# Four transformer layers on one core: the stores of the residual stream and of the output are begun from SyncE's queue instead of ScalarE's

## The chip, the cores and the metric

The kernel runs on one core of a Trainium2 chip. A core has five engines that work side by side: PE (TensorE, matrix products), DVE (VectorE), ACT (ScalarE), POOL (GpSimd) and SP (SyncE, which computes nothing and only begins transfers). A transfer between the chip's memory and a core's on-chip memory is begun by an instruction on the queue of SP, ACT or POOL, and is carried out by 16 DMA engines that all queues share. Each engine's queue runs in order: an instruction that waits holds up everything queued behind it on that engine.

The metric is the time of one execution in microseconds (us).

## The reference

Input `x` has 2048 rows (tokens) of 640 numbers, 32 heads of 20 numbers each. Two kinds of layer alternate, A B A B, and each adds its result to the residual stream `x`:

```python
x = A_x
x = x + _A_ref(_layernorm(x), A_wqkv, A_wo)          # linear attention
x = x + _B_ref(_layernorm(x), B_wq, ..., B_beta)     # segments with a memory
x = x + _A_ref(_layernorm(x), A_wqkv, A_wo)
x = x + _B_ref(_layernorm(x), B_wq, ..., B_beta)
# A: pq, pk = phi(q), phi(k); kv = pk^T v;  o = (pq kv) / (pq . sum(pk)), then @ wo
# B: per segment of 512 tokens and head
logits = qs @ ks^T * scale + mask;  a_dot = softmax(logits) @ vs
o = g * (pq @ M) / (pq . z) + (1 - g) * a_dot        # M, z: memory of earlier segments
M = M + pk^T vs;  z = z + sum(pk)                    # then o @ wo
```

## The kernel before, in words

The 2048 tokens are worked on in four segments of 512, and a segment in four tiles of 128 rows. The residual stream lives in the chip's memory: each layer loads a tile of it (`x` or `xo`), adds the layer's result into a new tile `xn`, and stores `xn`. A store is 128 x 640 numbers of 4 bytes, 320 KB, and there are 16 of them in each of the four layers, 64 in all. The last layer's 16 go to the output `out_x`, the other 48 to buffers that the next layer reads.

The stores stand in two places. In `a_second` (line 828, layers A, 32 stores) VectorE makes `xn` from the product in PSUM and the old `x` (line 479). In `b_out` (line 976, layers B, 32 stores) ScalarE copies the product (line 476) and GpSimd adds the old `x` (line 477); only for the last segment of the last layer does VectorE do both at once. Both stores use the queue `q_x`:

```python
self.o_half(oT[i], wo, "B", x, xn, n, later=not st.get("ends"))
...
self.q_x.dma_start(dst[r:r + P], xn)
```

Two streams of work are woven together. `dense` makes the projections, the residual additions and the memory; `attention` goes through the heads of layer B in groups of four, eight groups to a segment, 32 to a layer, 64 in the kernel. A group's work is spread over three slots: `row_max` (scores, then row maxima on VectorE, line 1013); `split_max` and `max_rows`, which turn the maxima into rows (transposed on PE in line 1031, copied by ScalarE into `mt` in line 1033) and send them by two small transfers into the query stack `qs` (line 1036, a pair of 4 KB transfers on SyncE's queue); then `scores` (PE in line 1048, exponential on ScalarE in line 1052, causal mask on GpSimd in line 1059) and `weigh` (PE, line 1075). The scores of a group cannot begin before its row pair has landed. The stacks `qs` and `ks` of the next group are loaded a group ahead (`stacks`, line 993), also on SyncE's queue.

PE's order of work is written out by hand: `run` steps the two streams by a planned cost, and `MANUAL = ("PE",)` keeps PE's instructions as they were written. The order on the other engines and queues is laid out when the program is built, by estimated times and dependencies.

Which queue begins which transfer is set by one tuple. Its six entries are, in order: the stored queries of layer A (`q_pq`), the stores of the residual stream and of the output (`q_x`), the queries and keys of layer B (`q_nat`), the row pair (`q_row`), the weights (`q_w`), and the reload of layer A's queries (`q_pqi`). Loads of the residual stream (line 330) and of the stacks (line 993) are on SyncE's queue in any case.

```python
self.q_pq, self.q_x, self.q_nat, self.q_row, self.q_w, self.q_pqi = [getattr(self.nc, e) for e in QUEUES]
```

Of the kernel before, what the change touches and what calls it, by code (L numbers as in the profile page):

```python
# [142 lines left out]
class Kernel:  # L143
    def __init__(self, ctx, tc, A, const, out):
# [7 lines left out]
        self.rate = 1.0  # L152
        self.q_pq, self.q_x, self.q_nat, self.q_row, self.q_w, self.q_pqi = [getattr(self.nc, e) for e in QUEUES]

# [1170 lines left out]

ROWS = 11
PQ = 5
QUEUES = ('gpsimd', 'scalar', 'sync', 'sync', 'gpsimd', 'sync')
PE_BUFS = 10
MANUAL = ("PE",)  # L1330
_INS = ["A_x", "A_wqkv", "A_wo", "B_wq", "B_wk", "B_wv", "B_wo", "B_beta"]
# [31 lines left out]
```

## Time and profile before

| what | value |
|---|---|
| median of three runs | 1738.13 us (1735.6 to 1741.74) |
| the profiled execution's own time | 1736.07 us |
| its span, first to last instruction | 1734.4 us |
| granted TensorE clock | 0.998 |
| PE busy | 1666.1 us, 96% |
| ACT busy | 969.7 us, 56% |
| transfers | 187.58 MB, 108 GB/s over the span |

The profile comes from one execution. "Busy" is the time in which an engine worked; the sequencer's own instructions (starting transfers, waiting on semaphores) are not counted in it and are shown with a q behind the engine's name: SPq, ACTq. L976 is line 976 of the kernel. In a row of the timeline stand the start, the duration, the engine, the line, the operation, what is written and read, how many instructions were merged, and in brackets the idle time before it with what ended it. In a row of windows stand the window, its length, PE's busy time in it, the granted clock, the DMA engines' busy share and GB/s. In a row of one source line stand the engine, the operation, the count, the shortest, median and longest duration in ns, and the first and last start in us. In a row of waits stand the total, the number of times and the longest.

### The profile page before, as it was taken

What the parts mean: (1) busy time and instruction counts of PE and PEld (TensorE: products, weight loads), DVE (VectorE), ACT (ScalarE), POOL (GpSimd) and SP (SyncE); (2) the same over time, 40 slices, a digit from 0 to 9 for tenths busy, and PEclk for the clock granted to TensorE, in tenths of its full rate; (3) what the DMA queues carried; (4) which work ended last, traced back from release to release, by engine and by line L of the source; (5) the groups of instructions that cost most, each with busy time, mean ns of one, the idle gap of its engine ahead of it and who ended that gap; (6) DMA issues with size and microseconds to landing.
All of it is one profiled execution on the core that took longest, in us unless ns stands there. A gap on an engine that the chain in (4) does not pass through costs nothing.

```text
span 1734.4 us, 36014 instructions
## 1 busy us (share of the span) xinstructions
PE 1666.1 (96%) x13032; PEld 1047.5 (60%) x13032; DVE 1180.9 (68%) x3849; ACT 969.7 (56%) x1818; POOL 517.7 (30%) x982
## 2 busy tenths in 40 slices
PE   6999999999999999999999999999999999999998
PEld 4676667664565576556556777666546545645555
DVE  8645534577787677759864456746777877878773
ACT  5545433357557645667675544333665576666673
POOL 1543350012123312334351301221422432233452
PEclk9999999999999999999999999999999999999999
DMA  7522452422322322352211303423232323223432
GB/s 262 184 109 95 150 195 97 139 76 82 113 71 73 113 96 68 120 179 95 78 48 51 103 32 122 175 98 116 75 102 85 112 81 108 93 82 111 131 115 92
DMA packets 118330, 187.58 MB, mean 108 GB/s; under 512 B 13949, under 2 KB 79613, under 8 KB 115849
## 3 DMA queue, kind: packets, MB, share of 16 engines
q1 hardware_dynamic: 105896, 142.68, 25.5%
q0 software_dynamic: 3040, 21.63, 3.4%
q10 hardware_dynamic: 9216, 20.98, 3.1%
q8 instruction: 103, 1.69, 0.4%
q14 instruction: 75, 0.61, 0.1%
HBM read 106.05 MB, written 78.64 MB: 106 GB/s over the span
## 4 chain that ended last, share of the span: by engine, by line
PE 78%; DVE 10%; ACT 6%; issue 2%; POOL 2%; DMA 1%; SPq 1%; ACTq 0%; POOLq 0%; DVEq 0%
PE ps L395 32%; PE ps L381 17%; PE ps L1075 7%; PE ps L1048 4%; ACT pe L1052 3%; PE ps L1007 3%; PE ps L319 3%; PE ps L564 3%; PE ps L450 3%; DVE ps L1013 2%; PE ps L1088 1%; PE ps L891 1%; PE ps L730 1%; DVE st L338 1%; DVE xn L479 1%
## 5 line engine op out<-in xcount | busy, mean ns | idle before, releaser
L1013 DVE CUSTOM_DVE_ANT_0 ps<-ps,maskw 128x512 f32<-128x512 f32 (+3 forms) x1024 | 472.5, 519 | 38.0 <-PE ps L1007 35.7
L1052 ACT ACTIVATE pe<-ps,lsc 128x512 f32<-128x512 f32 x640 | 394.8, 696 | 87.6 <-PE ps L1048 84.9
L1059 POOL TENSOR_SCALAR_AFFINE_SELECT pe<-pe 128x256 f32<-128x256 f32 (+1 forms) x640 | 229.7, 365 | 449.2 <-ACT pe L1052 444.0
L395 PEld LDWEIGHTS <-xT 128*128 128x128 f16 x2880 | 280.3, 98 | 114.6 <-issue 9.3
L395 PEld LDWEIGHTS <-oT 128*128 128x128 f16 x1920 | 185.7, 98 | 80.5 <-issue 7.0
L1075 PE MATMUL ps<-pe,v 128*32 128x512 f32 (+3 forms) x2048 | 162.2, 436 | 11.5 <-POOL pe L1059 5.1
L395 PE MATMUL ps<-w_Bo,oT 128*128 128x320 f16 x960 | 142.3, 302 | 2.8 <-ACT pe L1052 1.1
L1013 DVE DVE_READ_ACCUMULATOR2_ANT mg<- 128x1 f32 x1024 | 143.9, 141 | 0.0
L381 PE MATMUL ps<-xT,w_Bq 128*128 128x512 f16 x600 | 140.2, 380 | 1.9 <-ACT pe L1052 0.8
L395 PE MATMUL ps<-w_Bv,xT 128*128 128x320 f16 x960 | 139.7, 300 | 0.8 <-DVE otok L1095 0.6
L381 PE MATMUL ps<-xT,w_Bk 128*128 128x512 f16 x600 | 138.8, 380 | 1.2 <-ACT pe L1052 1.2
L395 PE MATMUL ps<-w_Ak,xT 128*128 128x320 f16 x960 | 136.1, 300 | 0.0
L1007 PE MATMUL ps<-ks,qs 60*128 60x512 f16 (+3 forms) x1024 | 123.1, 298 | 6.7 <-ACT pe L1052 2.9
L856 DVE SCALAR_TENSOR_TENSOR nat<-ps,nat 128x512 f16<-128x512 f32 x80 | 55.2, 690 | 89.2 <-ACT nat L855 89.1
L1048 PE MATMUL ps<-qs,ks 62*128 62x512 f16 (+3 forms) x1024 | 105.9, 301 | 3.0 <-DMA qs<-mt 1.5
L1075 PEld LDWEIGHTS ps<-pe,v 128*32 128x32 f32 x2048 | 65.3, 109 | 71.9 <-issue 45.8
L421 POOL TENSOR_SCALAR e<-e 128x320 f32<-128x320 f32 (+1 forms) x52 | 82.9, 1594 | 82.4 <-ACT e L417 78.2
L855 ACT ACTIVATE nat<-ps 128x512 f16<-128x512 f32 x80 | 48.2, 603 | 91.8 <-PE ps L381 69.2
L381 PEld LDWEIGHTS <-w_Bk 128*128 128x128 f16 x600 | 57.3, 98 | 65.5 <-issue 5.6
L381 PEld LDWEIGHTS <-w_Bq 128*128 128x128 f16 x600 | 56.7, 98 | 65.9 <-issue 7.8
L1007 PEld LDWEIGHTS <-qs 60*128 60x128 f16 x1024 | 50.0, 94 | 70.9 <-issue 44.7
L343 POOL TENSOR_TENSOR rs<-rs,mhalf 128x1 f32<-128x1 f32 x48 | 27.0, 563 | 218.8 <-DVE rs L342 218.7
(217 smaller groups left out, 2630.7 us busy)
## 6 DMA issues: line engine op xcount, KB each, us to landing
x<-xn ACTq DMA_DIRECT2D x48, 320.0 KB
qs<-qd SPq DMA_DIRECT2D x128, 120.0 KB
ks<-kd SPq DMA_DIRECT2D x128, 120.0 KB
xo<-x SPq DMA_DIRECT2D x48, 320.0 KB
pqi<-pqd SPq DMA_DIRECT2D x32, 320.0 KB
qd<-nat SPq DMA_DIRECT2D x40, 256.0 KB
kd<-nat SPq DMA_DIRECT2D x40, 256.0 KB
x<-in_A_x SPq DMA_DIRECT2D x16, 320.0 KB
```

The source lines that it names most:

```text
L319: nc.tensor.transpose(pt[:, (c - c0) * P:(c - c0 + 1) * P], src[:, c * P:(c + 1) * P], self.ident)
L381: nc.tensor.matmul(p, w[:, c, a, t * P:(t + 1) * P], xT[:, c, b, :], start=k == 0, stop=k == 3 * C - 1)
L395: nc.tensor.matmul(p, xT[:, c, a, i * P:(i + 1) * P], w[:, c, b, n * HN:(n + 1) * HN], start=k == 0, stop=k == 3 * C - 1)
L421: nc.gpsimd.tensor_scalar(e, e, 1.0, eps, op0=OP.min, op1=OP.add)
L450: nc.tensor.matmul(nd[:, lo - k * cut:hi - k * cut], pq[t], mem[:, OFF[t] + lo - a:OFF[t] + hi - a], start=first, stop=True, skip_group_ch ...
L856: nc.vector.scalar_tensor_tensor(nat[:, 1], p, QK_SHIFT, nat[:, 0], op0=OP.mult, op1=OP.subtract)
L1007: nc.tensor.matmul(bs[par][:, a:a + n], qs[r, p, i * P:(i + 1) * P], ks[r, p, :n], start=True, stop=True)
L1013: nc.vector.tensor_tensor_reduce(bs[par][:, a:a + n], bs[par][:, a:a + n], self.maskw[:, SEG - n:], 1.0, NEG, OP.add, OP.max, G["mg"][:, p ...
L1048: nc.tensor.matmul(b[:, a:a + n], ks[r, p, j * P:(j + 1) * P], qs[r, p, j * P:], start=True, stop=True)
L1052: nc.scalar.activation(e, b, AF.Exp, scale=self.lsc)
L1059: nc.gpsimd.affine_select(d, d, pattern=pat, compare_op=OP.is_ge, fill=0.0, base=0, channel_multiplier=-1)
L1075: nc.tensor.matmul(G["pv"][32 * h4:32 * h4 + 32, j * P:], v[j][:, h * E1:h * E1 + 32], G.pop((p, par, j)), start=j == 0, stop=j == 2, skip ...
```

## The change

One entry of the tuple goes from `'scalar'` to `'sync'`. The 64 stores are begun by SyncE, from the queue that also carries the loads, the queries and keys of layer B and the row pairs.

```diff
 ROWS = 11
 PQ = 5
-QUEUES = ('gpsimd', 'scalar', 'sync', 'sync', 'gpsimd', 'sync')
+QUEUES = ('gpsimd', 'sync', 'sync', 'sync', 'gpsimd', 'sync')
 PE_BUFS = 10
 MANUAL = ("PE",)
```

## The prediction

> **What bounds the kernel now.** I read the head of the profile page first: busy times, DMA queues, the chain of work that ended last, and the issues of the tensors whose store is moved.
>
> ```profile
> span 1734.4 us, 36014 instructions
> PE 1666.1 (96%) x13032; PEld 1047.5 (60%) x13032; DVE 1180.9 (68%) x3849; ACT 969.7 (56%) x1818; POOL 517.7 (30%) x982
> ...
> q1 hardware_dynamic: 105896, 142.68, 25.5%
> ...
> q10 hardware_dynamic: 9216, 20.98, 3.1%
> ...
> PE 78%; DVE 10%; ACT 6%; issue 2%; POOL 2%; DMA 1%; SPq 1%; ACTq 0%; POOLq 0%; DVEq 0%
> ...
> x<-xn ACTq DMA_DIRECT2D x48, 320.0 KB
> out_x<-xn ACTq DMA_DIRECT2D x16, 320.0 KB
> ```
>
> PE is busy 96% of the span; 1734.4 - 1666.1 = 68.3 us is all that it does not work. The change touches no matmul, so 68.3 us is the whole room for a gain. ScalarE's queue (ACTq) has 0% of the chain that ended last, SyncE's queue (SPq) 1%. The 64 stores are the only 20.98 MB on q10: 64 x 320 KB agrees, so q10 is ScalarE's row of DMA work and q1 is SyncE's, which already carries 142.68 MB.
>
> The profiled execution took 1736.07 us, its span 1734.4; the median of the runs is 1738.13, 2.06 above it, and the three runs lie 6 us apart. About 0.3%, 5.2 us, is what a measurement of this kernel can tell from no change, and "the same" means that below.
>
> **What a store costs on ScalarE.** Next come the stores by source line, and the timeline of one of them on four engines.
>
> ```profile
> L828 ACTq DMA_DIRECT2D x<-xn x32: 325/326/369, 261.8 to 1496.6; - x32
> L976 ACTq DMA_DIRECT2D x<-xn x16: 326/326/359, 556.7 to 978.2; - x16
> L976 ACTq DMA_DIRECT2D out_x<-xn x16: 338/338/374, 1608.6 to 1731.2; - x16
> ```
>
> ```profile
> 717.60 1.27 ACT L1052 ACTIVATE pe<-ps,lsc 128x512 f32<-128x512 f32 x2
> 718.79 0.33 ACTq L976 DMA_DIRECT2D x<-xn  x1
> 719.22 0.27 ACT L1033 ACTIVATE mt<-pm 32x128 f16<-32x128 f16 x1 [0.35 <-POOL pe L1059]
> 719.51 1.28 SPq L1036 DMA_DIRECT2D qs<-mt  x2
> 717.80 0.96 POOL L477 TENSOR_TENSOR xn<-xn,xo 128x320 f32<-128x320 f32 x1 [2.95 <-ACT xn L476]
> 722.90 0.61 PE L1048 MATMUL ps<-qs,ks 62*128 62x512 f16 x4
> ```
>
> The store begins at 718.79, right after GpSimd's add ended (717.80 + 0.96 = 718.76). It takes 0.33 us of ScalarE's sequencer, not of its datapath. The activation behind it starts at 719.22 although the one before had ended at 717.60 + 1.27 = 718.87: 0.35 us of ScalarE are lost, and the row pair on SyncE's queue (the row maxima that the scores need) begins 0.35 us later than it could. PE reads those rows at 722.90 and shows no wait there.
>
> **Part one, what leaves ScalarE.** 64 stores at 326 to 338 ns (their medians) are 32 x 0.326 + 16 x 0.326 + 16 x 0.338 = 21.1 us of issuing. What counts is only what PE later waits for. So I asked for PE's busy time in the 3 us behind each store that has 3 us behind it (63 windows; two of them and the sum are shown).
>
> ```profile
> 1636.21:1639.21 3.00, 1.18 (x9) 0.96 0.85 302
> 1674.44:1677.44 3.00, 1.92 (x16) 1.00 0.77 286
> sum 189.00, PE 182.67; mean PE 2.90
> ```
>
> In all 63 windows PE is idle 189.00 - 182.67 = 6.33 us. That is the upper bound of a direct gain. Two windows hold 1.82 + 1.08 = 2.90 us of it. There I looked at ScalarE and PE:
>
> ```profile
> 1635.50 0.69 ACT L1052 ACTIVATE pe<-ps,lsc 128x512 f32<-128x512 f32 x1
> 1636.21 0.34 ACTq L976 DMA_DIRECT2D out_x<-xn  x1
> 1636.65 1.84 ACT L1052 ACTIVATE pe<-ps,lsc 128x512 f32<-128x512 f32 x3 [0.46 <-ACT pe L1052]
> 1638.04 0.52 PE L319 MATMUL ps<-ident,ol 128*128 128x128 f32 x3 [1.91 <-ACT pe L1052]
> 1674.88 1.84 ACT L1052 ACTIVATE pe<-ps,lsc 128x512 f32<-128x512 f32 x3 [0.44 <-PE ps L319]
> ```
>
> At 1636 the exponentials stop for 0.46 us around the store and PE waits 1.91 us for them, so the store's share is 0.46 us; at 1674 the stop is 0.44 us before the same kind of group. I take 0.46 + 0.44 = 0.9 us as the gain, rounded. The other 61 windows share 3.43 us, mostly pieces too small to tie to a store, and I leave them as the upper end. In the places like 718.79 the 0.35 us come free ahead of a row pair for which PE does not wait, so nothing is gained there.
>
> **Part two, what SyncE gets.** The same 64 issues go to a queue that runs in order and also carries the loads and the row pairs. A store there costs about what it costs on ScalarE: the nearest row on SyncE's queue with the same 320 KB is a load, first row below. 64 x 0.369 = 23.6 us of issuing, spread over the kernel. What can be hurt is the row pair, since it alone is made and used within a few microseconds.
>
> ```profile
> L330 SPq DMA_DIRECT2D xo<-x x48: 319/369/1077, 533.3 to 1713.8; - x48
> L1036 SPq DMA_DIRECT2D qs<-mt x128: 610/617/699, 359.5 to 1695.8; - x128
> PE ps L1048 <- DMA qs<-mt: 1.5, 1, 1.5
> ```
>
> There are 64 pairs (128 transfers), and PE waited for one of them once, 1.5 us. How much slack is left? Here are the tightest pair of the whole run, and the one pair that PE waited for, the latter in the chain's own order of time:
>
> ```profile
> 1558.85 1.29 SPq L1036 DMA_DIRECT2D qs<-mt  x2
> ...
> 1561.55 0.61 PE L1048 MATMUL ps<-qs,ks 62*128 62x512 f16 x4
> ```
>
> ```profile
> 702.84 0.28 ACT mt L1033
> 703.11 0.02 issue
> 703.13 5.26 DMA qs<-mt
> ```
>
> Undisturbed, a pair has landed 1561.55 - 1558.85 = 2.70 us after its first issue (or earlier, PE shows no wait). At 703.13 it took 5.26 us; 1600 KB of weights are being fetched there on GpSimd's queue. So the pair is sensitive to what shares the DMA engines with it.
>
> Eight of the 64 pairs begin within 0.75 us behind a store, the first of them at 557.38 and the last at 1695.18:
>
> ```profile
> 556.66 0.33 ACTq L976 DMA_DIRECT2D x<-xn  x1
> 557.38 1.30 SPq L1036 DMA_DIRECT2D qs<-mt  x2
> ...
> 1694.84 0.34 ACTq L976 DMA_DIRECT2D out_x<-xn  x1
> 1695.18 1.27 SPq L1036 DMA_DIRECT2D qs<-mt  x2
> ```
>
> Another six begin 1.6 to 4.5 us behind one. Of the eight, the pair at 719.51 has the least slack, 722.90 - 719.51 = 3.39 us: 0.69 us more than 2.70. Three terms act on each of the eight. The activation that makes the rows no longer stands behind the store: 0.35 us earlier. The store's issue now stands ahead of the pair: 0.33 to 0.37 us later. These two cancel. The third is the transfer itself: q10's 3.1% of 1734.4 us over 64 stores is 0.84 us of all 16 engines for each store. It shared the engines with the pair before, on another queue; now it stands ahead of the pair on the same one. Bound from below: nothing, since the same bytes compete today and PE shows no wait at these eight. Bound from above: the whole 0.84 us, which passes the 0.69 us of slack by 0.15 us, or 8 x 0.15 = 1.2 us. I take the upper end, 1.2 us, because the pair at 703.13 shows that competition is felt.
>
> [...]
>
> The other transfers that follow a store are stack loads for the next group and loads of the residual. They are asked for a group ahead; the 64 pairs, one for each group, lie (1695.8 - 359.5) / 63 = 21 us apart on average (a stretch without attention included), and 0.4 us in front of such a load costs nothing. If that cover went, each would cost what the pair costs. The last store of all waits for the last VectorE instruction wherever it is begun, and its issue is as long there, so the tail keeps its length.
>
> **The sum.** 1736.07 - 0.9 + 1.2 = 1736.4 against the profiled execution, +0.3 us; against the median, 1738.4 us. Between the bounds: from -6.3 to +1.2.
>
> **Rivals.**
> *SyncE held at a store (slower).* A queue that runs in order stops at a store whose data is not there. Today ScalarE stands still for that. If a store is queued on SyncE ahead of a row pair and GpSimd's add (0.96 us in the row at 717.80) has not ended when the queue reaches it, the pair waits for the add, the issue and the transfer: 0.96 + 0.37 + 0.84 - 0.69 of slack = 1.48 us, and PE with it. For the eight close pairs that is 11.8 us, 1750; with the six farther ones 14 x 1.48 = 20.7 us, 1759. It decides as soon as a pair comes more than 0.69 us later than today. For it: eight pairs are this close, and the pair is the only transfer with no slot of lead. Against it: in today's order each of these stores has its data before the pair is ready.
>
> *The order of the other engines is drawn anew (either side).* Only PE's order is written by hand; VectorE's, ScalarE's, GpSimd's and SyncE's are laid out when the program is built, from estimated times, and the moved stores change those for every engine. How much the order is worth can be estimated from PE's busy time in fifteen 100 us stretches from 200 to 1700 (the two extremes and the sum):
>
> ```profile
> 200.00:300.00 100.00, 100.00 (x694) 1.00 0.38 130
> ...
> 1200.00:1300.00 100.00, 93.63 (x757) 1.00 0.27 85
> ...
> sum 1500.00, PE 1454.71; mean PE 96.98
> ```
>
> PE idles 3.0 us in a mean stretch, from 0 to 6.4, and a stretch lies 1.7 us from the mean (standard deviation of the fifteen). Fifteen stretches drawn anew would move the sum by 1.7 x 3.9 = 6.6 us either way, so about 1731.5 or 1745. For it: ScalarE's relief and SyncE's load both enter the estimate. Against it: 64 of 36014 instructions move, and most stretches may keep their order.
>
> *All direct gain (faster).* If every idle stretch behind a store is due to it, 6.3 us go: 1738.1 - 6.3 = 1731.8. Against it: at 1636 only 0.46 of 1.91 us are the store's.
>
> *It does nothing.* If the stores' queue does not matter at all the time is 1738.1; this lies inside the forecast.
>
> **How the numbers follow.** The forecast, within 0.3%, has 0.45. The held queue has 0.20. The new order has 0.28, split 0.10 faster and 0.18 slower, since an order that puts a store at the wrong place of a tight queue costs more than the freed ScalarE can return (6.3 us at most). The full gain has 0.07. That makes faster 0.17, same 0.45, slower 0.38. The likeliest case's own range is 1733 to 1743.3. The range over the cases goes from 1731.0, just below the full gain, to 1757.0, which holds the eight-pair price and most of the fourteen-pair one.
>
> **What would show it.** Right: no issue of these stores on ScalarE's queue, q10 gone or empty with q1 near 163.7 MB, the exponentials at about 1636 without the 0.46 us stop, PE's wait for the row transfers still about 1.5 us in total, PE's idle time within 5 us of 68.3. Wrong: a total of several microseconds in PE's wait for the row transfers, or row pairs that start late after their activation (0.02 us today, 703.11 above), would show the held queue. Idle PE time that moves between stretches without a store nearby would show the new order. A time over 1743.3 or under 1732.9 makes the forecast wrong.

## The result: 1.4% slower, and the profile after

The changed kernel takes 1763.22 us (median; 1761.84 to 1765.2) against 1739.49 us before: a ratio of 1.014, 95% interval 1.0117 to 1.0162. Forecast was 1738.4, with a range to 1757. The profiled execution took 1761.84 us, its span 1760.1.

The head of the page after, in the same order as before:

```profile
span 1760.1 us, 35958 instructions
PE 1676.5 (95%) x13032; PEld 1054.3 (60%) x13032; DVE 1181.7 (67%) x3849; ACT 969.1 (55%) x1818; POOL 517.7 (29%) x982
...
q1 hardware_dynamic: 115112, 163.66, 27.8%
...
PE 78%; DVE 8%; ACT 6%; DMA 3%; issue 2%; POOL 2%; SPq 1%; ACTq 0%; POOLq 0%; DVEq 0%
...
x<-xn SPq DMA_DIRECT2D x48, 320.0 KB
```

The change did what it says: q10 is gone and q1 carries 163.66 MB. The span grew by 25.7 us. PE is idle 1760.1 - 1676.5 = 83.6 us instead of 68.3, 15.3 more, and the same 13032 matmuls keep it busy 10.4 us longer. Transfers (DMA) have 3% of the chain that ended last instead of 1%. PE's waits name which ones (total, times, longest):

```profile
PE ps L450 <- DMA pqi<-pqd: 17.1, 4, 5.8
...
PE ps L319 <- DMA ol<-od: 3.7, 1, 3.7
...
PE ps L1048 <- DMA qs<-mt: 1.1, 1, 1.1
```

The first two rows do not stand among the waits of before: 20.8 us in five waits. `pqi` is the reload of layer A's stored queries (line 762), `ol` the load of attention output that was spilled to memory (line 961). The row pairs (`qs<-mt`), which the prediction watched, are waited for 1.1 us, less than the 1.5 before. PE's other idle time is 20.8 - 15.3 = 5.5 us shorter. Of this, 1.91 us lie at the fifth wait: it stands in front of the very matmul for which the kernel before waited 1.91 us for the exponentials (1638.04 in the prediction), so there only 1.8 of the 3.7 us are added. Here is the first of the five waits in the chain of the changed kernel, in order of time:

```profile
261.38 2.05 PE ps L395 x15
...
263.45 0.56 DVE xn L479
264.01 0.02 issue
264.03 0.33 SPq L828
...
264.46 4.66 DMA pqi<-pqd
269.12 0.14 issue
269.26 3.15 PE ps L450 x12
```

Read it backwards. PE's matmul of line 450 waits for the reload; the reload was issued at 264.46 because SyncE had been at the store of line 828; the store began at 264.03 because VectorE's `xn` ended at 264.01. That store had been at the head of SyncE's queue for 20.8 us, the longest of this row of SyncE's waits:

```profile
SPq L828 <- DVE xn L479: 184.3, 26, 20.8
```

In the kernel before, the timelines of SyncE, ScalarE and PE at the same place show the reload long gone when the store begins:

```profile
246.74 0.52 SPq L762 DMA_DIRECT2D pqi<-pqd  x1
...
261.84 0.37 ACTq L828 DMA_DIRECT2D x<-xn  x1
...
261.05 1.62 PE L450 MATMUL ps<-mem,pqi 128*128 128x147 f32 x12
```

The reload was issued 14.3 us before its first reader and 15.1 us before the store. In the other three segments the lead on the reader was 7.9 to 9.4 us. With the store on SyncE's queue, the order laid out at build time puts the store ahead of the reload, and all of that lead is lost; the other three stores hold the queue for 7.3 to 9.4 us. It happens once in each of the four segments of the first layer A, because there the code reaches the reload of tile 3 in the step after tile 0's store; in the other layer A it reaches it in the step of tile 0, ahead of that store.

The fifth wait has the same form. The last store of the first segment in the last layer waits for GpSimd's `xn`, and the load of spilled output, which the code reaches behind that store, waits with it:

```profile
1660.67 0.36 SPq L976
...
1661.08 3.08 DMA ol<-od
1664.16 0.14 issue
1664.30 0.52 PE ps L319 x3
```

Apart from the 64 stores, SyncE begins the same 775 transfers in both kernels, in the same order but for one place where three neighbours change turns. The stores were put in among them, and at all five places the store is also ahead of the load in the code.

The 10.4 us of longer work are TensorE's clock. PE's busy time in each quarter of a microsecond, times the share of the clock that was not granted, adds up to 14.1 us in the changed kernel and 3.4 before. Of the 14.1 us, 9.0 lie behind the four waits for the reload. The 1.7 us behind the fifth wait are not new: before, the 1.91 us of idle ahead of the same matmul cost as much. Another 1.6 us are new but come at 156, earlier than any of the 64 stores. PE in windows of 4 us around the first wait in the changed kernel (window, length, PE busy, granted clock, DMA share, GB/s):

```profile
260.00:264.00 4.00, 3.41 (x26) 1.00 0.90 336
264.00:268.00 4.00, 0.00 (x0) 0.72 0.91 292
268.00:272.00 4.00, 2.74 (x12) 0.50 0.20 72
272.00:276.00 4.00, 4.00 (x30) 0.92 0.00 0
```

PE stops at 263.4, the clock is halved within the second window, and the twelve matmuls of line 450 take 3.15 us where they take 1.62 us in the row of before. PE works again from 269.26, and the 0.92 of the last window puts full clock at about 272.6, 3.4 us later. Behind the other four waits it came back 4.4 to 6.0 us after PE resumed. The five waits are 3.5 to 5.8 us long.

### The profile page after: what moved, and what is told of

The parts are those of the page before. It is cut to its first block, busy times and chain, and to the rows that moved or that the text cites. A ratio compares the mean times of both kernels' runs of the same rounds, so it can differ in the third digit from the quotient of the medians.

```text
span 1760.1 us, 35958 instructions
## 1 busy us (share of the span) xinstructions
PE 1676.5 (95%) x13032; PEld 1054.3 (60%) x13032; DVE 1181.7 (67%) x3849; ACT 969.1 (55%) x1818; POOL 517.7 (29%) x982
## 3 DMA queue, kind: packets, MB, share of 16 engines
q1 hardware_dynamic: 115112, 163.66, 27.8%
## 4 chain that ended last, share of the span: by engine, by line
PE 78%; DVE 8%; ACT 6%; DMA 3%; issue 2%; POOL 2%; SPq 1%; ACTq 0%; POOLq 0%; DVEq 0%
PE ps L395 32%; PE ps L381 17%; PE ps L1075 7%; PE ps L1048 4%; PE ps L1007 3%; PE ps L450 3%; ACT pe L1052 3%; PE ps L319 3%; PE ps L564 3%; PE ps L1088 1%; DVE ps L1013 1%; PE ps L891 1%; PE ps L730 1%; DMA pqi<-pqd 1%; PE ps L883 1%
## 5 line engine op out<-in xcount | busy, mean ns | idle before, releaser
L1075 PE MATMUL ps<-pe,v 128*32 128x512 f32 (+3 forms) x2048 | 162.3, 436 | 12.7 <-POOL pe L1059 5.1
L1048 PE MATMUL ps<-qs,ks 62*128 62x384 f16 (+3 forms) x1024 | 107.0, 302 | 2.1 <-DMA qs<-mt 1.1
```

Of the source, the lines that this page charges most:

```text
L1048: nc.tensor.matmul(b[:, a:a + n], ks[r, p, j * P:(j + 1) * P], qs[r, p, j * P:], start=True, stop=True)
L1075: nc.tensor.matmul(G["pv"][32 * h4:32 * h4 + 32, j * P:], v[j][:, h * E1:h * E1 + 32], G.pop((p, par, j)), start=j == 0, stop=j == 2, skip ...
```

## The experiments

Theory 1: SyncE's queue runs in order, and five loads (four reloads, one spilled output) stand behind a store that waits for its data. Theory 2: the stores' bytes, ahead of other transfers on the same queue, cost the time. Theory 3: the order of the other engines was laid out anew and is worse.

**Four stores back on ScalarE.**

```diff
# the changed kernel, a_second
-            self.q_x.dma_start(dst[r:r + P], xn)
+            (nc.scalar if i == 0 and io == "A" else self.q_x).dma_start(dst[r:r + P], xn)
```

> All stores on SyncE's queue as in the change, except four: the store of the first tile of each segment in the first layer A, begun by ScalarE as before. Theory 1 (SyncE's queue runs in order; in each segment of the first layer A the reload of the stored queries stands behind the first tile's store, which waits for its data): the four waits of PE for that reload, 17.1 us in the changed kernel, fall below 1 us, the lowered TensorE clock behind them goes with them, and the time falls from 1763 to 1735 to 1743. Theory 2 (the 320 KB transfers stand ahead of other transfers on the same queue and cost bandwidth in order): 60 of 64 stores still do so, 1755 or more. Theory 3 (the order of VectorE, ScalarE and GpSimd was drawn anew and is worse): that order stays as in the changed kernel, so 1755 or more.

Measured: 1738.41 us, ratio to before 0.9997 (0.9987 to 1.0008). The reload has no row among PE's waits any more; the spilled output still has one. PE's busy time, and its remaining wait for a load:

```profile
PE 1670.2 (96%) x13032; PEld 1049.0 (60%) x13032; DVE 1180.5 (68%) x3849; ACT 968.5 (56%) x1818; POOL 517.7 (30%) x982
...
PE ps L319 <- DMA ol<-od: 3.8, 1, 3.8
```

At the four places the clock now stays at 1.00 (at the first in every window of 4 us from 256 to 288); the 4.1 us by which PE is busy longer than before lie elsewhere (half clock at 156, at 1372 and, behind the spilled output, at 1642; the mean clock of this execution is 0.995). The order of VectorE's, GpSimd's and ScalarE's computing instructions is exactly that of the changed kernel, which differs from that of before (VectorE's at 91 of 3849 places). So the new order of these engines costs nothing that can be measured: theory 3 falls. Sixty stores on SyncE's queue cost nothing that can be measured either.

**Only those four stores moved.**

```diff
# the kernel before, a_second
-            self.q_x.dma_start(dst[r:r + P], xn)
+            (nc.sync if i == 0 and io == "A" else self.q_x).dma_start(dst[r:r + P], xn)
```

> The kernel before with only those four stores (first tile of each segment in the first layer A) begun by SyncE; the order on VectorE and GpSimd is exactly that of before. Theory 1: four waits for the reload of the stored queries, 15 to 18 us in sum, and the time 1739 plus 20 to 30, so 1759 to 1769. Theory 2: 4 of 64 transfers, at most 1743. Theory 3: the order is that of before, 1736 to 1743.

Measured: 1761.31 us, ratio 1.0132 (1.0115 to 1.0148). PE's waits and the head of its page:

```profile
PE ps L450 <- DMA pqi<-pqd: 17.3, 4, 6.2
```

```profile
PE 1678.8 (95%) x13032; PEld 1055.4 (60%) x13032; DVE 1182.3 (67%) x3849; ACT 971.1 (55%) x1818; POOL 519.6 (30%) x982
```

Four of 64 stores make nearly the whole loss: 17.3 us of waiting, and PE busy 1678.8 - 1666.1 = 12.7 us longer, of which 8.9 us are half-clock work behind the four waits (mean clock 0.84, 0.84, 0.84 and 0.92 in a window of 22 us at each, 1.00 in the same windows of before). The order on VectorE, GpSimd and ScalarE and of SyncE's other 775 transfers is that of before. The two runs together show that the four stores are needed for the loss and are enough for nearly all of it.

**The wait without the bytes.** The four places again, in the kernel before, whose stores all stay on ScalarE.

```diff
# the kernel before, a_second; the helper `mark`, which makes the buffer, is left out
+            if i == 0 and io == "A":
+                self.nc.sync.dma_start(self.mark(dst)[r:r + P], xn[:, D - 4:])
```

> The kernel before, all its stores on ScalarE, and added four tiny transfers on SyncE's queue (4 numbers of each of the 128 rows, to a buffer that nobody reads) at the places of the four stores, each of which waits for the same new tile. It has the wait without the bytes. Theory 1: four waits of PE for the reload, 12 to 18 us in sum, and 1755 to 1768. Theory 2 (bytes): at most 1744.

Measured: 1769.73 us, ratio 1.0175 (1.0159 to 1.019).

```profile
PE ps L450 <- DMA pqi<-pqd: 23.3, 4, 7.5
```

Theory 1 is confirmed in kind, and its size was missed: 23.3 us instead of 12 to 18, and 1769.73 us where at most 1768 was expected. With 2 KB ahead of it on its queue instead of 320 KB the reload landed later, not sooner; the chain has 6.34 us for the first one, where the changed kernel has 4.66:

```profile
262.87 0.34 SPq L830
...
263.31 6.34 DMA pqi<-pqd
```

In this run the real store of 320 KB goes out on ScalarE's queue at the same time (262.88). Whether that or the tiny rows written ahead of it slow the reload was not tried and stays open.

**The bytes without the wait.**

```diff
# the kernel before, a_second; the helper `mark` is left out
+            if i == 0 and io == "A":
+                self.nc.sync.dma_start(self.mark(dst, D)[r:r + P], x)
```

> The kernel before, all its stores on ScalarE, and added four transfers of 320 KB on SyncE's queue at the same four places, of the old tile of the residual that has long landed, to a buffer that nobody reads. It has the bytes without the wait for the new tile. Theory 1: no wait of PE for the reload over 1 us, at most 1744. Theory 2 (bytes): the waits come back in part, 1750 or more.

Measured: 1738.56 us, ratio 0.9999 (0.9989 to 1.0008). SyncE's timeline at the first place, then at the second with PE's reading of the reload:

```profile
244.03 0.33 SPq L830 DMA_DIRECT2D mark<-xo  x1
247.31 0.52 SPq L762 DMA_DIRECT2D pqi<-pqd  x1
...
341.22 0.32 SPq L830 DMA_DIRECT2D mark<-xo  x1
341.63 0.52 SPq L762 DMA_DIRECT2D pqi<-pqd  x1
...
346.97 1.70 PE L450 MATMUL ps<-mem,pqi 128*128 128x147 f32 x12 [0.33 <-DVE mg L1021]
```

The 320 KB stand ahead of the reload in the queue, and at the first place the reload goes out at 247.3, 0.6 us later than before. At the second place they are begun only 0.41 us ahead of it, and PE reads it 5.3 us later without waiting for it. No row of PE's waits names it. Theory 2 falls: it is the wait, not the bytes. The reload keeps a lead of several microseconds in this run; what the bytes would cost a load with no lead is not shown by it.

**The reload on another queue.**

```diff
# the changed kernel
-QUEUES = ('gpsimd', 'sync', 'sync', 'sync', 'gpsimd', 'sync')
+QUEUES = ('gpsimd', 'sync', 'sync', 'sync', 'gpsimd', 'scalar')
```

> The change, and the reload of the stored queries in layers A begun from ScalarE's queue instead of SyncE's. In the order laid out at build time the fourth reload of each segment then stands on ScalarE behind the normalisation of the first tile, which needs the same data that the store needs. Theory 1 (what hurts is standing in order behind the first tile's data, on whichever queue): the four waits stay, 14 to 25 us in sum, and the time is 1755 or more. Theory 2 (what hurts is sharing SyncE's queue with the stores): the reload has a queue of its own, the four waits go and the time is 1745 or less. Theory 3: 1755 or more, with no wait for the reload.

Measured: 1770.88 us, ratio 1.019 (1.0172 to 1.0207); PE waits 24.1 us for the reload. The chain at the first place:

```profile
263.50 0.56 DVE xn L479
...
265.70 0.22 DVE nb L345
265.92 0.03 issue
265.95 0.02 ACT xh L368
265.97 0.04 issue
266.01 4.20 DMA pqi<-pqd
```

Now the reload stands behind ScalarE's normalisation of the same tile, which needs more steps than the store, so it goes out at 266.01, 1.55 us later than in the changed kernel. Leaving SyncE's queue does not help a transfer that on the other queue still stands behind the same data.

**All 64 on SyncE, each store behind the next tile's loads.**

```diff
# the changed kernel, a_second; b_out likewise
             x = self.load_x(src, s, i, "xo")
+            if late:
+                with self.tc.issue_after(self.loaded.ins):
+                    self.q_x.dma_start(*late.pop())
...
-            self.q_x.dma_start(dst[r:r + P], xn)
+            late.append((dst[r:r + P], xn))
...
+        self.q_x.dma_start(*late.pop())        # behind the loop over the tiles
```

> All 64 stores on SyncE's queue, but each store is begun only behind the next tile's loads (in layers A the reload of the queries and the load of the residual, in layers B the two loads of the next tile). Theory 1: the loads no longer stand behind a store that waits, PE's waits for the reload of the queries and of the spilled output fall below 1 us, 1733 to 1745. Theory 2: the same bytes on the same queue, 1755 or more. Theory 3: the order of the other engines is drawn a third time, anything from 1730 to 1770.

Measured: 1742.85 us, ratio 1.0018 (1.0006 to 1.0029). The reload's waits are gone, as theory 1 has it. The expectation for the spilled output failed; PE waits 4.0 us for it. SyncE there, in this kernel:

```profile
1637.41 0.36 SPq L987 DMA_DIRECT2D out_x<-xn  x1
1637.82 0.43 SPq L965 DMA_DIRECT2D ol<-od  x1
```

The store ahead is a segment's last one, which this edit does not put behind the first load of the next segment.

**Five stores back on ScalarE.** The four and that last store.

```diff
# on top of the first experiment, b_out
-            self.q_x.dma_start(dst[r:r + P], xn)
+            (nc.scalar if i == NT - 1 and s == 0 and not norm else self.q_x).dma_start(dst[r:r + P], xn)
```

> All stores on SyncE's queue except five, which ScalarE begins: the four of the first tile of each segment in the first layer A, and the last store of the first segment in the last layer, behind which a load of spilled output stood. Theory 1: PE's wait for the spilled output, 3.8 us with four stores back, falls below 1 us, its lowered clock goes too, and the time is 1731 to 1738, at or a little below that of before. If the other 59 stores cost something on SyncE after all, it stays at 1738 or above. Theory 2: the same within 2 us as with four stores back, 1736 to 1741.

Measured: 1736.02 us, ratio to before 0.998 (0.9971 to 0.999); the wait for the spilled output is shorter, but not below 1 us:

```profile
PE ps L319 <- DMA ol<-od: 1.5, 1, 1.5
```

It is the matmul that waited 3.8 us with four stores back, and 1.91 us for the exponentials in the kernel before. The time lies in the ranges of both theories and does not tell them apart. This version is 0.2% faster than the kernel before; whether ScalarE's freed time makes the difference was not measured by itself.

## Why the prediction was wrong, point by point

- *What bounds the kernel.* Right: PE does. But a cost was left out of the sum altogether: behind each of the five waits the clock fell to half. In the changed kernel 10.4 of the 25.7 us are work at a lowered clock, 9.0 of them behind the four waits for the reload. The trace of before had shown it: behind the 1.91 us idle at 1636, which the prediction quotes, these windows of before have the clock at half.

```profile
1638.00:1640.00 2.00, 1.97 (x12) 0.74 0.59 233
1640.00:1642.00 2.00, 2.00 (x10) 0.50 0.00 0
1642.00:1644.00 2.00, 2.00 (x24) 0.91 0.00 0
```

- *Part one, 0.9 us from ScalarE.* Right in sign at most: 60 stores moved give 0.9997, 59 moved give 0.998. The upper end, 6.3 us, was never reached. At the place where the forecast expected 0.46 of the 1.91 us back, the exponentials' stop is gone, but the same matmul then waits for the spilled output: 3.7 us with all 64 stores moved, 3.8 with 60, 1.5 with 59.
- *Part two, the row pairs.* The term of +1.2 us did not appear: PE's wait for them went from 1.5 to 1.1 us.
- *Part two, the other transfers.* This is the step that failed: "They are asked for a group ahead", so delay in front of them "costs nothing". That holds for the stack loads, which no row of PE's waits names. The sentence names the loads of the residual too and leaves out the reload of the queries and the spilled output; PE waited for the two left out 17.1 and 3.7 us. The lead was there, 7.9 to 14.3 us for the reload, but the store in front of it did not take 0.4 us of the queue; it held it for 7.3 to 20.8. I looked for what follows a store within 4.5 us in the order of before. What mattered was what was issued up to 15 us ahead of it, since on the shared queue the store stands in front of it.
- *The held queue as a rival.* Right mechanism, wrong place and price. The prediction gave it 0.20, priced it at 1.48 us for each of 8 to 14 row pairs, and would have reached 1750 to 1759. It was five loads at 3.5 to 5.8 us of waiting each, and the clock.
- *The argument against it*, "in today's order each of these stores has its data before the pair is ready", was about the row pairs and ScalarE's queue. On SyncE's queue the store is reached up to 20.8 us before its data is there.
- *The bytes of a store ahead on the same queue.* At the reloads they cost nothing that can be measured here (0.9999), so the upper end, 0.84 us of transfer for a store, was not seen. The four places tried are not those of the row pairs; there PE's shorter wait is all the evidence.
- *A new order of the other engines*, with 0.28, did not decide: the new order of VectorE, GpSimd and ScalarE ran at 0.9997.
- *It stays open* why the build places the store ahead of a load that the kernel before issued 15.1 us sooner than the store. It agrees with the order of the code at all five places; that the build goes by this in general was not tried.

## What to carry to other kernels

When a store moves to a queue that also issues loads, price the store as a wait for its data, not as 0.3 us of issuing, and list every load of that queue that could come to stand behind it, with its lead; here the five stood behind the store in the code, and the order of before did not show it. Where the order is laid out at build time, read it again after the change: here four stores of 64 made the loss, and putting five back gave a kernel slightly faster than both. Where PE is the bound, add to each idle of a few microseconds the half-speed work that can follow it: behind the five waits here it lost 1.7 to 3.0 us each.

## What the runs showed of the hardware that was not expected

Half the clock also followed a stop of PE that was shorter than the five waits of 3.5 to 5.8 us: behind the 1.91 us at 1636 in the kernel before, the clock fell about 2.8 us after the stop began (0.74 in the window 1638 to 1640) and 0.9 us after PE had resumed. One stop is not even needed: from 1089.8 to 1092.6 in the same kernel PE idled 1.9 us in four pieces of 0.30 to 0.68 us, and from 1092.8 the clock was at 0.50. But it does not always follow: in the kernel before PE stopped for 1.87 us at 153, and the clock stayed at 1.00 (windows from 152 to 163). What decides is not shown by these runs.

Behind the five waits of the changed kernel the clock fell 2.0 to 4.9 us after PE had stopped. Full clock came back 3.4 to 6.0 us after PE had resumed.

In the first segment the same 320 KB reload landed 4.66 us after its issue when 320 KB stood ahead of it on its own queue, and 6.34 us when only 2 KB did and the 320 KB went out on another queue at the same moment. Which of the two made it slower is open.
